# Channel mixing on one core: three of seven block products split once more, three parts per batch by turns, one batch's x in DRAM for a while

## The chip, the cores and the metric

The kernel runs on one core of a Trainium2 chip. The metric is the time of one execution in microseconds on the device. Three runs of the kernel before took 838.82, 838.87 and 838.88 us; the median is 838.87.

## The reference

The input is q, k and v of 4 batches, 8 heads, 768 positions and 64 elements a head, the centroids of 16 clusters per head, and four weights. Attention lets a query see only the keys of its own cluster. Its output, laid out as x of 768 × 512 per batch, goes through a token mixer and a channel mixer:

```python
xt = x.transpose(0, 2, 1)
h = np.maximum(xt @ w_tok1, 0.0) @ w_tok2      # w_tok1 768x256, w_tok2 256x768
u = x + h.transpose(0, 2, 1)
h2 = np.maximum(u @ w_ch1, 0.0) @ w_ch2        # w_ch1 512x1536, w_ch2 1536x512
return (u + h2).astype(np.float32)
```

## The kernel before

The program has three stages, and TensorE (PE) works through all of them.

**Attention** takes 16 steps, one for each pair of heads of a batch. Its code is the same in both kernels.

**Token stage.** It handles two batches at a time (0 and 1, then 2 and 3). `tok1(b, t)` makes the first token product and ScalarE (ACT) writes its relu into `h`. `tok2_chunks` makes the second one as a product of 2 × 2 blocks in Winograd's form: seven block products (p1, p5, c11, u2, c12, c22, c21) in place of eight. The names say which block of the result each completes; blocks A11 to A22 and their sums S1 to S4 are left factors, B11 to B22 and T1 to T4 right ones. Three chains of PSUM banks, X, Z and Y, gather the products, and VectorE (DVE) adds every bank to x after each product. In between, steps of other work are put by hand with `take`: rounding of the last weights (`weight_steps`: load on the SyncE queue SP, two ops on ACT, four on DVE), sums of weights (`left_chunk`), and the turning of u.

**Turning of u.** The channel stage needs u transposed. `u_take(b, i)` copies one of eight pieces of x on ACT into `urows` (L612) and issues a DMA transpose into `ucols` on SP (L614). `u_put(i)` copies the result into `uT` on ACT (L625). `urows` and `ucols` have two buffers each. `u_sums` then makes T1 to T4 of u on DVE.

**Channel stage.** It goes through the batches 0, 1, 2, 3. The 1536 hidden channels are two halves of six chunks of 128 (the rows of blocks of w_ch1), and u is two halves of 384 positions. For each batch there are two parts of three chunks. `ch1_chunk` makes the seven products of a chunk: each is two matmuls of 128 × 128 weights with 384 columns (L741). ACT copies p1, p5 and u2 out of PSUM (L749), DVE adds the later products to the copies (L536), ACT makes the relu, and DVE forms the sums S1 to S4 of the hidden values. `ch2_chunk` makes the second channel product from three chunks of hidden values: seven products of three matmuls with 256 columns each (L792), DVE adding seven times. `chunk` orders the seven products of both functions and leaves the last one, c21, to be made after the first product of the chunk that follows:

```python
        X = ptile("X", n)
        product(X, "A11", "B11", True)
        if late:
            late.pop()()
        done("p1", X)
```

In batch 0 the sums of the weights (`right_weights`, `left_chunk`) are made between the chunks, and `fits` prepares a check of the value range. Every instruction order is the order of the program: nothing is rescheduled. X and Z have three PSUM banks each, Y has two.

A matmul on f32 data appears in the trace as two passes, each with its weight load.

Of the kernel before, what the change touches and what calls it, by code (L numbers as in the profile page):

```python
# [8 lines left out]
F32 = mybir.dt.float32  # L9
# [10 lines left out]
P = 128  # L20
# [16 lines left out]
EX = 9  # L37
SM_SCALE = 0.125
# [10 lines left out]
def kernel(  # L49
# [46 lines left out]
    tokens = fast.enter_context(ExitStack())  # L96
    tokpool = pool("tokpool", 1, tokens)
# [31 lines left out]
    xs = [xpool.tile([P, NJ, DM], F32, name=f"x{b}") for b in range(B)]  # L129
# [401 lines left out]

    def sub(dst, a, b):
        nc.vector.tensor_tensor(out=dst, in0=a, in1=b, op=ALU.subtract)
# [17 lines left out]
    def left_sums(A, part):  # L551
        a = {name: part(x) for name, x in A.items()}
        yield lambda: add(a["S1"], a["A21"], a["A22"])
        yield lambda: sub(a["S2"], a["S1"], a["A11"])
        yield lambda: sub(a["S3"], a["A11"], a["A21"])
        yield lambda: sub(a["S4"], a["A12"], a["S2"])

    def left_chunk(c):
        return left_sums(pools["A"], lambda x: x[:, :, c * P : (c + 1) * P])

    def token_weights():
# [8 lines left out]
        return left_sums(A, lambda x: x)  # L570
# [15 lines left out]
    def right_weights(part):  # L586
# [12 lines left out]
        b = {name: x[:, 3 * part : 3 * part + 3] for name, x in pools["B"].items()}  # L599
# [7 lines left out]
    def u_take(b, i):  # L607
# [3 lines left out]
        rows = pools["u"].tile([P, 2, HJ, P], U16, name="urows", bufs=2)  # L611
        nc.scalar.copy(out=rows, in_=x.rearrange("p j (c w) -> p w j c", w=2))  # L612
        cols = pools["u"].tile([P, 2, HJ, P], U16, name="ucols", bufs=2)
# [13 lines left out]
    def u_steps(b):  # L627

        N = 2 * NF
        for i in range(2):  # L630
            yield lambda i=i: u_take(b, i)
        for i in range(N):
            yield lambda i=i: (u_put(i), i + 2 < N and u_take(b, i + 2))

    def u_sums(half):
        if half == 0:
            uT = pools["uT"]
            uTs = pools["uTs"] = pools["u"].tile([P, 3, NF // 2, HS], F32, name="uTs")
            R = pools["R"] = {
                f"B{i + 1}{j + 1}": uT[:, j, 2 * i : 2 * i + 2] for i in range(2) for j in range(2)  # L640
            }
            R["T1"], R["T2"], R["T4"] = (uTs[:, i] for i in range(3))
            R["T3"] = R["B12"]
            sub(R["T1"], R["B12"], R["B11"])
            sub(R["T2"], R["B22"], R["T1"])
        else:
            R = pools["R"]
            sub(R["T3"], R["B22"], R["B12"])
            sub(R["T4"], R["B21"], R["T2"])

    late, outs = [], []

    def chunk(n, product, done, last):

        X = ptile("X", n)
        product(X, "A11", "B11", True)
        if late:
            late.pop()()
        done("p1", X)
        Z = ptile("Z", n)  # L660
        product(Z, "S1", "T1", True)
        done("p5", Z)
        Y = ptile("Y", n)

        def product_y():
            product(Y, "A12", "B21", True)
            done("c11", Y)

        def product_z():
            product(Z, "S4", "B22", False)  # L670
            done("c12", Z)


        between = [product_y, product_z]
        if not last:
            between.pop(0)()
        product(X, "S2", "T2", False)
        done("u2", X)
        between.pop(0)()
        product(X, "S3", "T3", False)  # L680
        done("c22", X)
        if last:
            between.pop(0)()

        def end():
            product(X, "A22", "T4", False)
            done("c21", X)

        late.append(end)

    def tok2_chunks(b, half):


        A, R = pools["AT"], pools["RT"]
        kinds = {
            "p1": ("X", "A11", "B11", "c11"),
            "p5": ("Z", "S1", "T1", "c22"),
            "c11": ("Y", "A12", "B21", "c11"),
            "u2": ("X", "S2", "T2", "c12"),
            "c12": ("Z", "S4", "B22", "c12"),  # L700
            "c22": ("X", "S3", "T3", "c22"),
            "c21": ("X", "A22", "T4", "c21"),
        }

        def product(name, i):
            tag, a, r, to = kinds[name]
            start = name in ("p1", "p5", "c11")
            if start:
                banks[tag, i] = ptile(tag, DM)
            nc.tensor.matmul(  # L710
                banks[tag, i], lhsT=A[a][:, i], rhs=R[r], start=start, stop=True,
                skip_group_check=not start,
            )
            x = xs[b + int(to[2]) - 1][:, HJ * (int(to[1]) - 1) + i]
            add(x, banks[tag, i], x)

        orders = (
            (("p1", "012"), ("p5", "012"), ("c11", "01"), ("u2", "012"), ("c12", "01")),
            (("c22", "012"), ("c12", "2"), ("c11", "2"), ("c21", "012")),
        )  # L720
        if half == 0:
            pools["banks"] = {}
        banks = pools["banks"]
        for name, chunks in orders[half]:
            for i in chunks:
                product(name, int(i))

    def ch1_chunk(part, i):

        c = 3 * part + i  # L730
        if i == 0:
            pools["h2"] = {
                k: pools["mlp"].tile([P, 3, HS], F32, name="h" + k)
                for k in ("A11", "A12", "A22", "S1", "S2", "S3", "S4")
            }
        A, R, h2 = pools["A"], pools["R"], pools["h2"]
        kept = {}

        def product(psum, a, r, start):
            for k in range(2):  # L740
                nc.tensor.matmul(  # L741
                    psum, lhsT=A[a][:, k, c * P : (c + 1) * P], rhs=R[r][:, k],
# [3 lines left out]
        def done(name, psum):  # L746
            if name in ("p1", "p5", "u2"):
                kept[name] = pools["mlp"].tile([P, HS], F32, name=name, bufs=2)
                nc.scalar.copy(out=kept[name], in_=psum)  # L749
            elif name == "c11":  # L750
                a = h2["A11"][:, i]
                add(a, psum, kept["p1"])
                nc.scalar.activation(out=a, in_=a, func=ACT.Relu)
            elif name == "c12":
                kept["c12"] = pools["mlp"].tile([P, HS], F32, name="c12", bufs=2)
                add(kept["c12"], psum, kept["u2"])
            elif name == "c22":
                a = h2["A22"][:, i]
                add(a, psum, kept["p5"])
                nc.scalar.activation(out=a, in_=a, func=ACT.Relu)  # L760

                nc.vector.scalar_tensor_tensor(
                    out=h2["S3"][:, i], in0=kept["c12"], scalar=0.0, in1=h2["A11"][:, i],
                    op0=ALU.max, op1=ALU.subtract,
                )
                nc.vector.scalar_tensor_tensor(
# [182 lines left out]
    for b in (0, 2):  # L949
# [17 lines left out]
        if b == 2:  # L967
            take(turning, 2)
# [11 lines left out]
        if b == 2:  # L980
            u_sums(0)
# [256 lines left out]
```

## Time and profile before

| | |
|---|---|
| median of three runs | 838.87 us |
| the profiled execution: its time, its span | 838.82 us, 837.0 us |
| busy: PE, weight loads, DVE, ACT | 827.9, 502.6, 518.4, 377.3 us |
| token stage, first `tok1` to last `tok2_chunks` | about 316.6 to 394.7 us |
| channel stage, PE | about 394.7 to 831.3 us |
| matmul pass of 384, 256, 512 columns, mean duration | 487, 379, 593 ns |
| granted TensorE clock | full speed |

The busy times are sums over one execution. A matmul's duration in the trace holds its way through the array as well, so passes overlap; the distance between the starts of two passes says what a pass costs. Lines such as L536 (`add`) and L533 (`sub`) belong to helpers, so the tiles tell which step is meant: `hA`, `hS` are hidden values, `uTs` sums of u, `w1s` and `w2s` sums of w_ch1 and w_ch2, `h1s` sums of the token stage's hidden values.

### The profile page before, as it was taken

How to read it: one execution, taken by the hardware profiler on the slowest of the kernel's cores; microseconds unless marked ns; L12 is line 12 of the kernel's file. 1: busy time of each engine (PE TensorE's matmuls, PEld its weight loads, DVE VectorE, ACT ScalarE, POOL GpSimd, SP SyncE). 2: the span in 40 equal slices, each digit the busy share in tenths (PEclk: the TensorE clock that was granted, in tenths of full speed). 3: DMA queues.
4: the chain of work that ended last, by engine and by line, in shares of the span. 5: the costliest groups of instructions: out<-in, count | busy, mean ns of one | idle time of the engine just before them, and what ended most of it. 6: DMA issues, size and time to landing. Idle time of an engine off the chain costs nothing.

```text
span 837.0 us, 10822 instructions
## 1 busy us (share of the span) xinstructions
PE 827.9 (99%) x4087; PEld 502.6 (60%) x4087; DVE 518.4 (62%) x908; ACT 377.3 (45%) x575; POOL 30.7 (4%) x28
## 2 busy tenths in 40 slices
PE   9999999999999999999999999999999999999997
PEld 4444444444444444444587686785866858768676
DVE  6879898989898878759644735424354234443342
ACT  5678677787877774054201352103612036120210
POOL 1001010101101000000000000000000000000000
PEclk9999999999999999999999999999999999999999
DMA  9886566867676335032000040001410012200001
GB/s 153 147 158 147 117 139 130 165 131 160 145 136 130 83 95 152 18 88 39 0 1 1 19 107 25 1 1 19 95 39 0 1 20 52 80 0 1 1 19 61
DMA packets 183965, 60.21 MB, mean 72 GB/s; under 512 B 172768, under 2 KB 176864, under 8 KB 183904
## 3 DMA queue, kind: packets, MB, share of 16 engines
q1 hardware_dynamic: 182304, 59.04, 33.5%
q8 instruction: 34, 0.56, 0.3%
q10 hardware_dynamic: 1600, 0.39, 0.2%
q14 instruction: 27, 0.22, 0.1%
HBM read 34.64 MB, written 6.29 MB: 49 GB/s over the span
## 4 chain that ended last, share of the span: by engine, by line
PE 93%; DVE 5%; issue 0%; DMA 0%; ACT 0%; SPq 0%; DVEq 0%; ACTq 0%
PE sc L414 17%; PE pX L792 15%; PE pX L741 14%; PE av L439 13%; PE pZ L741 8%; PE pZ L792 7%; PE ph L518 5%; PE pY L792 4%; PE pY L741 4%; PE pX L710 2%; PE small L475 1%; DVE sum L429 1%; PE pZ L710 1%; PE small L299 1%; DVE x L536 1%; PE pY L710 1%
## 5 line engine op out<-in xcount | busy, mean ns | idle before, releaser
L421 ACT ACTIVATE ex<-sc 128x768 f32<-128x768 f32 x192 | 151.0, 812 | 28.5 <-PE sc L414 16.9
L414 PE MATMUL sc<-qkT 64*128 64x384 f32 x768 | 155.0, 482 | 0.0
L429 DVE TENSOR_TENSOR sum<-sum,ex 128x768 f32<-128x768 f32 x128 | 127.8, 999 | 26.9 <-ACT ex L421 14.2
L439 PE MATMUL av<-ex,va 128*64 128x384 f32 x768 | 127.4, 488 | 0.0
L439 PEld LDWEIGHTS av<-ex,va 128*64 128x64 f32 x768 | 53.7, 137 | 71.7 <-issue 67.5
L414 PEld LDWEIGHTS sc<-qkT 64*128 64x128 f32 x768 | 67.9, 187 | 38.4 <-issue 38.3
L749 ACT COPY p<-pX 128x384 f32<-128x384 f32 x24 | 11.4, 475 | 134.9 <-PE pX L741 117.4
L741 PE MATMUL pX<-uT,wc 128*128 128x384 f32 x192 | 67.3, 487 | 0.2 <-DVE x L536 0.2
L414 PE MATMUL sc<-ohT 64*128 64x384 bf16 x384 | 62.7, 323 | 0.1
L536 DVE TENSOR_TENSOR x<-pX,x 128x512 f32<-128x512 f32 (+1 forms) x48 | 25.8, 553 | 44.3 <-PE pX L792 42.8
L741 PEld LDWEIGHTS pX<-uT,wc 128*128 128x128 f32 x192 | 36.3, 190 | 24.7 <-issue 1.0
L446 ACT COPY avrows<-av 128x768 uint16<-128x768 uint16 x32 | 25.5, 797 | 45.0 <-PE av L439 45.0
L536 DVE TENSOR_TENSOR c<-pZ,u 128x384 f32<-128x384 f32 x24 | 13.4, 558 | 47.3 <-PE pZ L741 47.3
L518 PE MATMUL ph<-x,wt 128*128 128x512 f32 x96 | 41.6, 593 | 0.0
L625 ACT COPY uT<-ucols 128x768 uint16<-128x768 uint16 x32 | 33.7, 1053 | 17.6 <-DMA ucols<-urows 17.5
L760 ACT ACTIVATE hA<-hA 128x384 f32<-128x384 f32 x24 | 12.5, 523 | 64.0 <-DVE hA L536 64.0
L414 PEld LDWEIGHTS <-ohT 64*128 64x128 bf16 x384 | 18.7, 94 | 34.3 <-issue 9.4
L741 PE MATMUL pZ<-uTs,w1s 128*128 128x384 f32 x96 | 35.3, 490 | 0.6 <-DVE w1s L536 0.2
L792 PE MATMUL pX<-w2s,hA 128*128 128x256 f32 x144 | 35.0, 379 | 0.0
L792 PE MATMUL pX<-wc,hA 128*128 128x256 f32 x144 | 35.0, 379 | 0.0
L792 PE MATMUL pZ<-w2s,hS 128*128 128x256 f32 x144 | 35.0, 379 | 0.0
L792 PE MATMUL pY<-wc,hA 128*128 128x256 f32 x144 | 35.0, 379 | 0.0
(139 smaller groups left out, 1214.3 us busy)
## 6 DMA issues: line engine op xcount, KB each, us to landing
raw<-in_moe_w_ch_dram SPq DMA_DIRECT2D x24, 512.0 KB, 4.6
va<-in_v_dram SPq DMA_DIRECT2D x16, 384.0 KB, 3.6
out_dram<-x SPq DMA_DIRECT2D x24, 256.0 KB, 2.3
qk<-in_k_dram SPq DMA_DIRECT2D x60, 96.0 KB, 3.8
qk<-in_q_dram SPq DMA_DIRECT2D x60, 96.0 KB, 3.6
raw<-in_moe_w_tok_dram SPq DMA_DIRECT2D x3, 512.0 KB, 4.3
raw<-in_moe_w_tok_dram SPq DMA_DIRECT2D x4, 384.0 KB, 3.9
ucols<-urows SPq DMA_TRANSPOSE x32, 2.8
```

The lines of the kernel that those rows point to most:

```text
L414: nc.tensor.matmul(sc[:, h, 0:HS], lhsT=src[rows, 1, j], rhs=src[rows, 0, js], start=start, stop=not start,)
L421: nc.scalar.activation(out=ex, in_=sc[:, :, 0:HS], func=ACT.Exp, scale=SM_SCALE)
L429: nc.vector.tensor_tensor(out=acc, in0=acc if j > 1 else st["ex", qh, 0], in1=st["ex", qh, j], op=ALU.add)
L439: nc.tensor.matmul(av[h * D : (h + 1) * D], lhsT=st["va"][:, h, j], rhs=ex[:, h], start=(j == 0), stop=(j == NJ - 1),)
L446: nc.scalar.copy(out=st["rows"][:, qh], in_=av.bitcast(U16).rearrange("p (t w) -> p w t", w=2))
L518: nc.tensor.matmul(pf, lhsT=W["tok1"][:, j, t * P : (t + 1) * P], rhs=xs[b][:, j], start=(j == 0), stop=(j == NJ - 1),)
L536: nc.vector.tensor_tensor(out=dst, in0=a, in1=b, op=ALU.add)
L625: nc.scalar.copy(out=out, in_=pools.pop(("ucols", i)).rearrange("p w j t -> p w (j t)"))
L710: nc.tensor.matmul(banks[tag, i], lhsT=A[a][:, i], rhs=R[r], start=start, stop=True, skip_group_check=not start,)
L741: nc.tensor.matmul(psum, lhsT=A[a][:, k, c * P : (c + 1) * P], rhs=R[r][:, k], start=start and k == 0, stop=k == 1, skip_group_check=not s ...
L760: nc.scalar.activation(out=a, in_=a, func=ACT.Relu)
L792: nc.tensor.matmul(psum, lhsT=h2[a][:, k, i * P : (i + 1) * P], rhs=Bw[w][:, 3 * part + k], start=start and k == 0, stop=k == 2, skip_grou ...
```

## The change

**Two levels.** The two chunks c and c + 3 of one half are now handled together (`ch1_pair`, with c = part). For every pair but the first of batch 0, three of the seven products, A12·B21, S4·B22 and A22·T4 (called Y, Z and X), are themselves 2 × 2 block products: the two blocks of channels are the two chunks, the inner blocks are the two 128-row halves, and the 384 positions are two times 192. Each is made of seven products of one matmul with 192 columns. The first-level left and right factors get second-level sums: `set_left_sums` (tile `w1ss`, in batch 0 for each part once) and `set_right_sums` (tile `uTss`, for each batch, eight DVE ops). The results are added on DVE to the hidden values, bank by bank; the other four products remain as they were.

**Three parts.** There are three parts per batch, each of one pair, where there were two of three chunks. The second channel product now has two matmuls for each of its products and is made three times per batch (`ch2_chunks`). `by_turns` takes the three rows of blocks by turns, for the token product and the second channel product alike; DVE adds each bank directly to x after each product, 21 times per part.

**Order of the rest.** Small steps (weight sums, second-level sums) come from the list `others`, one after each product (`between`). u is turned in the order 0, 1, 4, 5, 6, 7, 2, 3 with two `urows` and three `ucols`, three takes ahead. In the third part of a batch the next u is turned: three takes in `ch1_pair`, the rest after the fourth product of `ch2_chunks`; T1 follows after the sixteenth, and T2 to T4 and the second-level sums after the last. In the token stage three takes are issued at once where there were two, and `left_sums(0)` works on two chunks where `left_chunk(0)` had one.

**Memory.** The x of batch 1 lies in memory of the token stage. It is written to DRAM before the last `tok1`, and read back into the memory of batch 0's x after batch 0 is out. The channel stage takes the batches in the order 0, 2, 3, 1. The rows of a batch go out after its third part, for the last batch as each is done.

The core of the diff:

```diff
+UROWS, UCOLS = 2, 3
...
-    xs = [xpool.tile([P, NJ, DM], F32, name=f"x{b}") for b in range(B)]
+    spill = spilled.tile([P, NJ, DM], F32, name="spill")
+    xs = [(x1pool if b == 1 else xpool).tile([P, NJ, DM], F32, name=f"x{b}") for b in range(B)]
...
+    def set_lefts():
...
+        both = W["ch1"].rearrange("p f (i r c) -> p f i r c", i=2, r=2)[:, 2:4]
+        single = A["S4"].rearrange("p f (r c) -> p f r c", r=2)
...
+    def set_right_sums():
+        pools["r2"] = pools["w2sums"].tile([P, 3, 3, HS // 2], F32, name="uTss")
+        for blocks in set_rights():
+            yield from winograd_right(blocks)
...
+    def by_turns(n, product, of, done=None, last=False, after=()):
...
+            order = "p1 0 p1 1 p1 2 p5 0 p5 1 p5 2 c11 0 c11 1 u2 0 u2 1 u2 2 c12 0 c12 1 "
+            order += "c22 0 c22 1 c22 2 c12 2 c11 2 c21 0 c21 1 c21 2"
...
+            product(banks[tag, i], a, r, i, name in FIRST)
+            x = of(to, i)
+            add(x, banks[tag, i], x)
...
+            if m in after:
+                after[m]()
+            between()
...
+    def ch1_pair(part, sets, beside):
...
+        def big(psum, a, r, i, start):
+            product(psum, a, r, i, start)
+            between()
+            if a != "A11" and beside:
+                beside.pop(0)()
+
+        def set_(psum, which, name, start):
+            _, a, r, _ = SEVEN[name]
+            nc.tensor.matmul(
+                psum, lhsT=left[which][a][:, part * P : part * P + P], rhs=right[which][r],
+                start=start, stop=True, skip_group_check=not start,
+            )
...
+        def set_x(which, tag, name, x):
+            if tag:
+                chains[which] = ptile(tag, HS // 2)
+            bank = chains[which]
+            set_(bank, which, name, name == "p1")
+            add(x, both(bank) if len(x.shape) == 3 else bank, x)
...
+        if sets:
+            yc = ptile("X", HS)
+            set_(yc[:, n0], "Y", "c11", True)
+            set_(yc[:, n1], "Y", "c12", True)
+            add(a11[:, 0], yc, a11[:, 0])
+            set_x("Y", "Y", "p1", a11[:, 0, n0])
+        Z[1] = ptile("Z", HS)
+        big(Z[1], "S1", "T1", 1, True)
+        nc.scalar.copy(out=p5[:, 1], in_=Z[1])
+        if sets:
+            set_x("Y", None, "u2", a11[:, 0, n1])
+            set_z("Y", ptile("Y", HS // 2), a11)
...
+        big(X[1], "S3", "T3", 1, False)
+        add(a22[:, 1], X[1], p5[:, 1])
+        relu(a22)
+        if sets:
+            set_x("Z", None, "c22", c12[:, 1].rearrange("p (k t) -> p k t", k=2))
+            set_(X[0][:, n0], "X", "c11", False)
+            set_(X[0][:, n1], "X", "c12", False)
+            nc.scalar.copy(out=a12[:, 0], in_=X[0])
+            set_(X[1][:, n0], "X", "c21", False)
+            nc.scalar.copy(out=a12[:, 1], in_=X[1])
...
+            set_x("X", "Y", "p1", a12[:, 0, n0])
+            sum_1()
+
+            def late_1():
+                set_x("X", None, "u2", a12[:, 0, n1])
+                set_z("X", ptile("Z", HS // 2), a12)
+                sub(h2["S2"], h2["S1"], a11)
...
-            take(turning, 2)
+            take(turning, UCOLS)
             take(weights, 2)
...
-            take(list(left_chunk(0)), 4)
+            take(list(left_sums(0)), 4)
+            nc.sync.dma_start(spill, xs[1])
...
+    batches = (0, 2, 3, 1)
...
+            ch1_pair(part, not first, [turning.pop(0) for _ in turning[:UCOLS]])
...
+            if part == 2 and not last:
+                after[3] = lambda: take(turning, len(turning))
+                after[15] = lambda: next(usums)
+                usums = u_sums()
+            ch2_chunks(b, part, last, after)
+            between(len(others))
...
+            if part == 2 and not last:
+                for _ in range(3):
+                    next(usums)
+                for step in set_right_sums():
+                    step()
+                if n == 0:
+                    xs[1] = xpool.tile([P, NJ, DM], F32, name="x0")
+                    nc.sync.dma_start(xs[1], spill)
```

## The prediction

> **What bounds the kernel now.** I read the page first (shares, slices, chain), then the groups by shape, and then the timeline of each engine around the place where the token stage hands over to the channel stage.
>
> ```profile
> span 837.0 us, 10822 instructions
> ...
> PE 827.9 (99%) x4087; PEld 502.6 (60%) x4087; DVE 518.4 (62%) x908; ACT 377.3 (45%) x575; POOL 30.7 (4%) x28
> ...
> PE   9999999999999999999999999999999999999997
> ...
> PEclk9999999999999999999999999999999999999999
> ...
> PE 93%; DVE 5%; issue 0%; DMA 0%; ACT 0%; SPq 0%; DVEq 0%; ACTq 0%
> ```
>
> PE is busy from start to end at the full clock and is nearly the whole chain. A busy PE is not proof of a full one, so the starts decide:
>
> ```profile
> 396.11 1.45 PE L741 MATMUL pZ<-uTs,w1s 128*128 128x384 f32 x4
> 397.40 1.45 PE L741 MATMUL pY<-uT,wc 128*128 128x384 f32 x4
> ...
> 403.85 1.45 PE L741 MATMUL pX<-uTs,wc 128*128 128x384 f32 x4
> 405.45 1.56 PE L741 MATMUL pZ<-uTs,w1s 128*128 128x384 f32 x4
> 406.84 1.45 PE L741 MATMUL pY<-uT,wc 128*128 128x384 f32 x4
> ...
> 601.05 1.46 PE L792 MATMUL pZ<-wc,hS 128*128 128x256 f32 x6
> 602.34 1.46 PE L792 MATMUL pX<-wc,hS 128*128 128x256 f32 x6
> ```
>
> One f32 matmul of the program shows as two passes. Four passes of 384 columns take 1.29 us from start to start (322.5 ns each), six of 256 columns 1.295 (216 ns): 0.833 ns a column plus 2.5 ns. From batch 1 on no gap breaks this rhythm; in batch 0 four products wait for DVE sums of weights (the one at 405.45 comes 0.31 late, and its first pass takes 0.10 longer). So each nanosecond that PE streams less is won, and each new wait of PE is lost at once.
>
> **What the change takes from PE.** A pair of chunks (c, c+3) took 28 matmuls of 384. In 11 of the 12 pairs the three products A12·B21, S4·B22, A22·T4 (12 matmuls, 24 passes) now become 21 matmuls of 192 columns (42 passes). No row has that width with 128 weight columns; the two rows above give 192 × 0.833 + 2.5 = 162.5 ns. Away go 24 × 322.5 = 7.74 us, in come 42 × 162.5 = 6.83: 0.915 us a pair, **−10.07 us** in all. The listing agrees: 132 matmuls of 384 fewer, 231 of 192 more. The second channel product keeps its 504 matmuls.
>
> Can weights be loaded at that pace? The groups by shape (mean ns of one behind the comma):
>
> ```profile
> L741 PEld LDWEIGHTS pX<-uTs,wc 128*128 128x128 f32 x96 | 18.2, 190 | 11.0
> ...
> L536 DVE TENSOR_TENSOR hA<-pX,p 128x384 f32<-128x384 f32 x24 | 13.4, 558 | 15.9 <-PE pX L741 15.9
> ...
> L773 ACT ACTIVATE hA<-pX 128x384 f32<-128x384 f32 x24 | 11.8, 491 | 30.8 <-PE pX L741 30.8
> ...
> L536 DVE TENSOR_TENSOR x<-pX,p 128x256 f32<-128x256 f32 x24 | 10.2, 425 | 20.9 <-PE pX L792 20.9
> ...
> L533 DVE TENSOR_TENSOR uTs<-uT,uTs 128x768 f32<-128x768 f32 x8 | 7.6, 954 | 0.4
> ```
>
> A load lasts 190 ns, more than 162.5. If that were its occupancy, each of 11 × 42 passes would take 27.5 ns more, +12.7 us. But the late product at 405.45 paid only 0.10 us for an unhidden load before it streamed, so I take the load to occupy about 105 ns and to hide. The Trainium skill (TensorE: Matmul & The Clock Gate, "LDWEIGHTS (loading the stationary operand)") makes a load cost its columns divided by 1.2, an estimate of 107 ns for 128 columns: by the rule nothing is added, by the 190 ns row 12.7 us, and no run here shows which holds at 192 columns.
>
> **DVE and ACT prices.** DVE ops follow each other at 0.337 us (256 elements), 0.475 (384), 0.595 (512), 0.87 (768), by the starts of back-to-back adds; for 192 the same slope gives 0.27, lasting 0.36. One that needs the op before it waits about 0.12 longer. DVE or ACT starts 0.20 us after PE's last pass has streamed (402.56 to 402.76). PE streams 0.16 after what it waited for (0.05 to the weight load, 0.105 for it). In a pair with its second product DVE has some 21 us of work (21 adds of 256, 19 ops of 192 to 768) in 35 us of PE time (8 × 1.29 + 21 × 0.325 + 21 × 0.864): not a bound, but chains through it can be late.
>
> **Token stage, batches 2 and 3.** The timeline of ACT, then that of DVE (start, us, what; in brackets the wait before it):
>
> ```profile
> 361.18 1.55 ACT L612 COPY urows<-x 128x768 uint16<-128x768 uint16 x2
> ...
> 368.84 0.67 ACT L202 ACTIVATE wh<-raw 128x512 f32<-128x512 f32 x1 [2.45 <-DMA raw<-in_moe_w_ch_dram]
> ...
> 374.47 0.59 ACT L522 ACTIVATE h<-ph 128x512 f32<-128x512 f32 x1
> ```
>
> ```profile
> 375.09 0.69 DVE L533 TENSOR_TENSOR h1s<-h,h 128x512 f32<-128x512 f32 x1 [3.11 <-ACT h L522]
> ...
> 381.23 1.88 DVE L536 TENSOR_TENSOR x<-pX,x 128x512 f32<-128x512 f32 x3
> ...
> 395.71 0.94 DVE L533 TENSOR_TENSOR uT<-uT 128x768 f32<-128x768 f32 x1
> ```
>
> Now three take steps stand at 361.18 with two urows buffers, so the third copy waits for the first transpose to land: issued 362.03, 2.8 us, 364.83. Behind it on ACT stand the four weight roundings and the relus of h. On SP the two raw weight loads (364.68) stand behind the third transpose (about 365.7 plus 1.27 us issue): 367.0, +2.35. They landed 4.2 us after issue, so the later roundings and with them the relu at 374.47 and DVE's first token sum come 2.35 later. From 375.09 to 397.5 DVE has no gap of note: it sets the pace there. It also gets left_sums of 512 elements where there were 256: 4 × 0.26 = 1.04. The last token adds, whose banks the first channel products wait for, come **3.4 us** later. Bounds: 0 (ACT's wait absorbed) to 5 (loads slower behind three transposes).
>
> The spill (1.5 MB) stands on SP before the last three transposes. At the 434 GB/s that DMA reached between 367 and 368 us, during a raw load, it takes 3.6 us, at the attention stage's 150 GB/s 10. Those transposes feed T2 of u, which DVE reaches after 14 of 21 token products, some 12 us on; ACT has nothing else to do meanwhile. I take 0; with the cover gone, up to 3. The reload waits on SP for batch 0's six rows; the next transpose on SP is 70 us away: 0. Batch order, the later rows of the first three batches and the last row's way out (one 256 KB row after the last add, 2.3 us, as now) cost nothing, ±0.5.
>
> **First pair of batch 0** (old products). Its two A22·T4 products run between the first products of the second part, and those reuse their banks at once: 0.20 to ACT, 0.49 relu, 0.16 back to PE, 0.85 twice, +1.7. In return the four waits for weight sums go (0.31 to 0.37 plus 0.10 each, −1.7), since those sums are now spread between products. **0**; bounds −1.7 and +1.7.
>
> **Batch boundaries, three.** From the end of PE's last product of a batch DVE does that add (start +0.20, next op +0.53), T2, T3, T4 of u (2.61), eight set sums (4 × 0.475 + 4 × 0.27, two or three dependent waits: 3.2), and only at +6.3 the add of the first set bank; two dependent adds end at +7.29, so u2 of that chain can stream at +7.45. PE meanwhile has four large products and three set matmuls before that u2, 4 × 1.29 + 3 × 0.325 = 6.14 us; then it waits, and all later products wait behind it. Stall 1.31, **+3.9 us**; bounds 0.5 and 2 each. Today's boundary has only T1 to T4 there and no wait.
>
> **Within a pair.** The last chain is tight: after the second S3·T3 product 0.20, add 0.56, relu of 768 0.74, copy 0.49, add 0.36, 0.16 and four hand-overs of 0.03: 2.6. PE has five set matmuls and one second-part product, 5 × 0.325 + 0.864 = 2.49. About 0.08 each, **+0.9 us** over 11 pairs; bounds 0 and 0.4 each. The other chain links have 0.4 us or more of room. **Extra weight sums** in batch 0 (24 small DVE ops behind which bank adds queue): **+0.5**, bounds 0 and 2.
>
> Sum: −10.07 + 3.4 + 0 + 3.9 + 0.9 + 0.5 = −1.4. The profiled execution took 838.82 us (span 837.0 and 1.8 around it), the median of the three runs is 838.87; so 837.4.
>
> **Rivals.** (1) *The waits are mostly hidden*: the late token sums are caught up and the boundary costs 0.5 each: −10.07 + 1 + 1.5 + 0.9 + 0.5 = about −6 at best, −4 in the middle, 834.9. For it: DVE is only 62% busy. Against: both waits stand in one engine's own order. (2) *DVE's chains pace the pairs*, ending slower: every set bank is read by DVE before its next product may add to it. If a link of the last chain is 0.1 us longer and the boundary 0.5, it is 11 × 0.3 + 1.5 more, +3.4, 842. It decides once the links after S3·T3 add up to over 2.8 us. For it: the margin is already gone. (3) *The load of 190 ns binds*: −1.4 + 12.7, 850. Against: the 0.10 us of the late product. (4) *Fewer passes do not appear* (the new products replace others, or DMA for the spill takes PE's time): the listing excludes the first.
>
> **How the numbers follow.** About 0.2% (1.7 us) is what a measurement of this kernel can tell from no change. The sum as worked, 0.62, own range 835.4 to 839.6: the forecast lies just inside no change, so 0.24 of it is faster and 0.36 same, 0.02 slower. Rival 1, 0.18, nearly all faster. Rival 2, 0.14, slower with 0.03 same. Rival 3 and others, 0.06, slower. Together faster 0.42, same 0.39, slower 0.19. The range reaches to rivals 1 and 2 and leaves out rival 3: 833.9 to 841.6.
>
> **What would show it.** Right: 192-column passes 162 to 163 ns apart; PE's last stretch ending near 830; waits of PE near 380 (2 to 3 us, on DVE's x adds), three of 1.3 on hA adds at the batch changes, two of 0.85 on ACT in the first pair. Wrong: passes 190 apart, PE gaps of 0.3 or more in every pair, no wait near 380, or a tail longer than now's 6 us after PE.

## The result, and the profile after

The changed kernel takes 838.86 us (median of six runs, 838.69 to 839.02), the kernel before 838.85 beside it: a ratio of 1.0002, 95% interval 0.9989 to 1.0015. That is no difference that can be measured here. The profiled execution took 838.92 us with a span of 837.0; the forecast of 837.4 was 1.5 us too low.

The page of the kernel after, at the places shown of the kernel before (span; busy times; chain that ended last):

```profile
span 837.0 us, 11463 instructions
...
PE 820.4 (98%) x4285; PEld 526.1 (63%) x4285; DVE 606.3 (72%) x1124; ACT 381.3 (46%) x562; POOL 30.7 (4%) x28
...
PE 86%; DVE 7%; ACT 2%; DMA 2%; issue 1%; SPq 0%; ACTq 0%; DVEq 0%
```

PE is busy 7.5 us less in the same span, and its share of the chain fell from 93% to 86%: DVE, ACT and DMA have taken its place on the path. Where, the waits of PE from 370 us on say (engine, line <- releaser: us in total, times, longest):

```profile
PE pY L801 <- DVE hA L554: 3.3, 3, 1.1
PE pX L762 <- DVE x L554: 2.2, 2, 2.0
PE pX L940 <- ACT hA L925: 1.2, 2, 0.6
PE pX L788 <- DVE x L554: 0.5, 1, 0.5
PE pX L940 <- ACT hA L886: 0.4, 1, 0.4
PE pX L762 <- ACT h L527: 0.2, 1, 0.2
```

In this kernel L801 is a matmul of 192 columns, L788 one of 384, L940 the second channel product, L762 the token product, L554 the bank add, L925 the relu of the old-style pair. This view counts a wait from the modelled end of the pass before it. The distance of the starts gives the whole loss, as in PE's timeline after a change of batch:

```profile
512.22 0.49 PE L801 MATMUL pY<-uT,wc 128*128 128x192 f32 x2
512.54 1.45 PE L788 MATMUL pZ<-uTs,w1s 128*128 128x384 f32 x4
515.10 0.92 PE L801 MATMUL pY<-uTss,w1ss 128*128 128x192 f32 x4 [1.11 <-DVE hA L554]
515.85 1.45 PE L788 MATMUL pX<-uTs,w1s 128*128 128x384 f32 x4
```

Two passes of 192 columns take 0.325 us from start to start (512.22 to 512.54), 162.5 ns each, as forecast. Four passes of 384 take 1.29, so the product at 515.10 was due at 513.83: 1.27 late, and its four passes take 0.75 in place of 0.65. I take the 0.10 for a weight load that nothing hid: the first two loads start there at 515.10 and 515.21, although each row lasts 0.19. By such starts, the sum of the prediction against the trace:

| step | forecast, us | in the trace of after |
|---|---|---|
| stream, 11 pairs | −10.07 | passes 162.5 ns apart in every pair |
| token stage | +3.4 | first channel product at 398.27, before 394.75: +3.5, of which 0.13 come from attention, which ends later |
| first pair | −1.7 + 1.7 | the four waits on weight sums are gone; two waits of 0.74 + 0.10 on ACT |
| three batch changes | +3.9 | 3 × (1.27 + 0.10) = 4.1 |
| last chain of a pair | +0.9 | 10 × 0.06 = 0.6 (the eleventh pair is the row before the last) |
| extra weight sums | +0.5 | 0.31 + 0.10 at 465.03 and 0.06 at 458.89 |
| start of the last second product | – | 0.56 + 0.08, at 811.26 where 810.70 was due |
| tail after PE | 0 ± 0.5 | last DVE add to end of span 5.91, before 5.28: +0.6 |

PE's last pass starts at 830.22, before at 830.92, so 0.7 us were won on PE, and the tail gave 0.6 of them back. The two last rows of the table, 1.3 us that the forecast had at nothing, are the error; the other rows miss by 0.3 or less each, and these misses cancel.

The token stage's two parts stand in DVE's rows, first of the kernel before, then of the one after:

```profile
377.96 0.42 DVE L536 TENSOR_TENSOR w1s<-wc 128x256 f32<-128x256 f32 x1
...
379.42 0.68 DVE L533 TENSOR_TENSOR h1s<-h,h1s 128x512 f32<-128x512 f32 x1
```

```profile
377.55 0.69 DVE L551 TENSOR_TENSOR h1s<-h,h 128x512 f32<-128x512 f32 x1 [3.14 <-ACT h L527]
...
380.41 0.68 DVE L554 TENSOR_TENSOR w1s<-wc 128x512 f32<-128x512 f32 x1
...
382.94 0.68 DVE L551 TENSOR_TENSOR h1s<-h,h1s 128x512 f32<-128x512 f32 x1
...
384.75 1.88 DVE L554 TENSOR_TENSOR x<-pX,x 128x512 f32<-128x512 f32 x3
```

The first token sum starts 2.46 later than before (377.55, 375.09), 2.33 without the 0.13 of attention, where the forecast has 2.35. The sums of w_ch1 take 2.53 in place of 1.46, 1.07 more (forecast 1.04), and the first x add comes 3.52 later (384.75, 381.23).

### The profile page after: what moved, and what is told of

It is laid out like the page before. It is cut to its first block, busy times and chain, and to the rows that moved or that the text cites. A ratio compares the mean times of both kernels' runs of the same rounds, so it can differ in the third digit from the quotient of the medians.

```text
span 837.0 us, 11463 instructions
## 1 busy us (share of the span) xinstructions
PE 820.4 (98%) x4285; PEld 526.1 (63%) x4285; DVE 606.3 (72%) x1124; ACT 381.3 (46%) x562; POOL 30.7 (4%) x28
## 4 chain that ended last, share of the span: by engine, by line
PE 86%; DVE 7%; ACT 2%; DMA 2%; issue 1%; SPq 0%; ACTq 0%; DVEq 0%
PE sc L419 19%; PE av L444 14%; PE pX L940 13%; PE pX L788 11%; PE pZ L940 6%; PE pY L801 4%; PE pY L940 3%; PE ph L523 3%; PE pZ L788 3%; PE pZ L801 3%; DVE x L554 2%; PE pX L801 2%; DMA ucols<-urows 1%; PE small L480 1%; PE pX L762 1%
## 5 line engine op out<-in xcount | busy, mean ns | idle before, releaser
L554 DVE TENSOR_TENSOR x<-pX,x 128x256 f32<-128x256 f32 (+1 forms) x168 | 76.2, 459 | 41.2 <-PE pX L940 39.7
L828 ACT COPY hA<-pX 128x384 f32<-128x384 f32 x24 | 11.5, 479 | 147.8 <-PE pX L788 143.0
L554 DVE TENSOR_TENSOR hA<-pY,hA 128x192 f32<-128x192 f32 (+1 forms) x90 | 36.7, 408 | 54.1 <-PE pY L801 39.6
L810 ACT ACTIVATE hA<-hA 128x768 f32<-128x768 f32 x35 | 29.5, 844 | 87.1 <-DVE hA L554 87.1
L788 PE MATMUL pX<-uT,wc 128*128 128x384 f32 x192 | 68.0, 487 | 0.5 <-DVE x L554 0.5
L788 PEld LDWEIGHTS pX<-uT,wc 128*128 128x128 f32 x192 | 35.7, 190 | 18.3 <-issue 1.3
L554 DVE TENSOR_TENSOR x<-pZ,x 128x256 f32<-128x256 f32 (+1 forms) x84 | 36.4, 456 | 13.0 <-PE pZ L940 12.5
L940 PE MATMUL pX<-wc,hA 128*128 128x256 f32 x144 | 37.2, 381 | 1.6 <-ACT hA L925 1.2
L940 PE MATMUL pY<-wc,hA 128*128 128x256 f32 x144 | 35.1, 379 | 0.0
L940 PE MATMUL pZ<-wc,hS 128*128 128x256 f32 x144 | 35.0, 379 | 0.0
L788 PE MATMUL pX<-uTs,w1s 128*128 128x384 f32 x96 | 34.9, 486 | 0.0
```

Source lines behind the costliest of these rows:

```text
L554: nc.vector.tensor_tensor(out=dst, in0=a, in1=b, op=ALU.add)
L788: nc.tensor.matmul(psum, lhsT=A[a][:, k, c], rhs=R[r][:, k], start=start and k == 0, stop=k == 1, skip_group_check=not start,)
L810: nc.scalar.activation(out=x, in_=x, func=ACT.Relu)
L940: nc.tensor.matmul(psum, lhsT=h2[a][:, k, i * P : (i + 1) * P], rhs=Bw[w][:, part + 3 * k], start=start and k == 0, stop=k == 1, skip_grou ...
```

## The experiments

Each kernel is the changed one with one edit, unless said otherwise; times are medians, ratios are against runs of the kernel before on the same chip, whose medians lay between 838.56 and 838.85.

**Two takes first** (`e1_two_takes`).

```diff
-            take(turning, UCOLS)
+            take(turning, 2)
...
-                take(turning, 4)
+                take(turning, 5)
```

> The changed kernel, but with two take steps of u before the last weight roundings of the token stage, as before the change, and the third one after them. Theory (the gain of the stream is real and named waits give it back): the third urows copy no longer waits 2.14 us on ACT for the first transpose, the two raw weight loads are issued on SP about 2.4 us earlier (364.7 instead of 367.2), DVE's first token sum starts near 375.1 instead of 377.55, PE's wait of 2.17 near 382.9 all but vanishes, and the time falls by 2.2 to 2.5 us, to about 836.5. Rival: something else than this wait makes the token stage late (DVE's own queue, or the spill): the sums start earlier but PE's wait on the x adds stays, and the time falls by at most 1.2, to 837.7 or more. A second rival, that the stage is late because the loads themselves are slower: nothing moves, 838.9.

It took 837.38 us, ratio 0.9983 (0.9974 to 0.9992); the first channel product starts at 397.08, 1.2 earlier. That is the size of the first rival, and the reason is in the timelines of ACT and DVE:

```profile
375.00 0.83 ACT L684 COPY urows<-x 128x768 uint16<-128x768 uint16 x1 [0.28 <-DMA ucols<-urows]
375.74 1.10 ACT L527 ACTIVATE h<-ph 128x512 f32<-128x512 f32 x2
```

```profile
376.36 0.69 DVE L551 TENSOR_TENSOR h1s<-h,h 128x512 f32<-128x512 f32 x1 [4.29 <-ACT h L527]
```

The wait of 2.14 is gone and the roundings run 2.4 earlier (368.92 in place of 371.27), but the edit puts five steps of u between them and the relu, where the kernel before has four: one copy more (375.00), with its own 0.73 and a new wait of 0.28. So only half of the term went. With four steps there (the second line of the edit left out, in the kernel with all edits below) the sum starts at 375.20, 2.35 before the 377.55 of the changed kernel, which is the forecast's term.

**Sums of w_ch1 into DVE's gap** (`e2_left_sums_early`).

```diff
         tok1(b + 1, 0)
+        if b == 2:
+            left_weights()
+            take(list(left_sums(0)), 4)
         token_sums(b, 0)
...
-            left_weights()
-            take(list(left_sums(0)), 4)
             nc.sync.dma_start(spill, xs[1])
```

> The changed kernel, but the four sums of w_ch1 for the first part are issued on DVE just before the first token sum of batches 2 and 3 instead of behind it; DVE idles 3.14 us there. Theory: the four sums of 512 elements take 4 x 0.6 = 2.4 us out of the queue between the token sums and the x adds, PE's waits near 382.9 to 397.2 (together 3.9 us with their load shares) shrink, and the first channel product starts up to 2.4 us earlier: time about 836.5. Rival: ACT's relu of the hidden values is what is late and PE would wait for that in place of DVE: the channel stage starts at most 0.5 earlier, 838.4 to 838.9.

836.03 us, ratio 0.9968 (0.9956 to 0.9980). PE's wait of 2.17 (ahead of the pass at 385.49 in the changed kernel) is gone; one of 0.53 + 0.10 on ACT's relu, ahead of the pass at 377.90, and the small ones at the end of the stage (0.66 at most) stay. The theory holds: what stood in DVE's queue between the token sums and the x adds was on the path, all 2.4 us of it.

**The batch change** (`e3_boundary`). DVE's timeline there, in the changed kernel:

```profile
507.90 0.42 DVE L554 TENSOR_TENSOR x<-pX,x 128x256 f32<-128x256 f32 x1 [0.44 <-PE pX L940]
508.24 0.95 DVE L551 TENSOR_TENSOR uTs<-uT,uTs 128x768 f32<-128x768 f32 x1
...
513.77 0.35 DVE L551 TENSOR_TENSOR uTss<-uTs,uTss 128x192 f32<-128x192 f32 x1
514.03 0.55 DVE L554 TENSOR_TENSOR hA<-pX,hA 128x384 f32<-128x384 f32 x1
514.69 0.36 DVE L554 TENSOR_TENSOR hA<-pY,hA 128x192 f32<-128x192 f32 x1
```

From the last add of the batch (507.90) to the first add of a set bank (514.03) DVE works without a gap for 6.1 us, with the hand-over of 0.20 ahead of it the forecast's 6.3. The bank that waits there was complete at 512.22, and PE waits for the add at 514.69.

```diff
-                for _ in range(3):
-                    next(usums)
-                for step in set_right_sums():
-                    step()
+                next(usums)
+                sets = list(set_right_sums())
+                for step in sets[:4]:
+                    step()
+                next(usums)
+                pools["rest"] = [lambda u=usums, s=sets[4]: (next(u), s())] + sets[5:]
...
+        others.extend(pools.pop("rest", []))
         big(X[0], "S2", "T2", 0, False)
```

> The changed kernel, but at the three batch changes DVE makes T2, the four second-level sums that need no T, and T3 only; T4 and the four sums made of it follow one by one after the products of the next batch's first pair. Theory: about 2.3 us of DVE work leave the queue ahead of the first set-bank add, so the three waits of 1.27 + 0.10 us on that chain (513.5, 620.9, 728.3) vanish: 3 x 1.37 = 4.1 us, time about 834.8. Rival (DVE's chains pace the pairs): the work put off lands between the set-bank adds, and PE waits there instead: at most 1.5 us of the 4.1 are won, 837.4 or more, with new waits of 0.3 to 1 us on hA or c adds in these pairs.

In this order T3 and T4 read blocks of u that the second-level sums have already replaced, so the values differ from the reference's; the instructions and their sizes do not. 834.44 us, ratio 0.9949 (0.9936 to 0.9963), 4.1 us below the kernel before. The three waits are gone and no other has come. DVE's total work is the same as before the edit: it was its place that cost. (The kernel with all edits has an order that keeps the values: T2, T3, T4, two of the sums, the other six later.)

**The old-style pair** (`e4_first_pair`).

```diff
-            late.extend([lambda: late_(0), lambda: late_(1)])
+            late_(0)
+            late_(1)
```

> The changed kernel, but in the one pair that is made the old way the two products A22 x T4 are made at the end of the pair instead of between the first products of the second channel product. Theory: the two bank waits on ACT's relu (0.74 + 0.10 us each at 415.65 and 418.65) vanish since other products lie between the reading of a bank and its next use: 1.7 us, time about 837.2. Rival: the moved products wait for DVE's reading of the banks they add to, or the second channel product then waits for the hidden sums: the waits move and less than 0.6 is won, 838.3 or more.

836.97 us, ratio 0.9979 (0.9970 to 0.9988). Both waits are gone and none replaces them, so the two bank waits were worth the 1.7 us.

**The register loads** (`e6_check_load`). The wait before the last second product is put down to ACT's copy by the profile. The source view of line 988, where each engine loads the outcome of the range check into registers, and PE's timeline show what else stands there:

```profile
L988 PEldq TENSOR_LOAD <-count x3: 305/306/496, 809.9 to 810.9; - x3
```

```profile
810.37 0.49 PE L801 MATMUL pY<-uTs,wc 128*128 128x192 f32 x2
811.26 1.10 PE L940 MATMUL pX<-wc,hA 128*128 128x256 f32 x4 [0.40 <-ACT hA L886]
```

```diff
             nc.scalar.copy(out=a11[:, i], in_=X[i])
+        if load:
+            pools["both"] = fits_load()
...
-            if last:
-                both = fits_load()
```

> The changed kernel, but the three register loads by which each engine reads the result of the range check are issued in the last pair after its second product instead of after the pair. Theory: the wait of PE before the last second channel product (0.56 + 0.08 us at 810.5) is the three loads in PE's own queue (0.50, 0.31 and 0.31 us with 0.1 between, 1.33 together), which stood behind an instruction held by a semaphore until about 809.8 and had only about 0.8 us of issued work ahead of them; between two large products of 1.29 us they hide, the wait falls to the 0.06 of every other pair or to nothing, and the time falls by 0.5, to 838.4. Rival: the profile's releaser, ACT's copy of hA behind the long relu, is the cause: the wait stays, 838.9, or the loads hold PE at the new place for up to 0.6.

838.19 us, ratio 0.9994 (0.9985 to 1.0003). The interval alone doesn't tell it from no change; the trace does (L942 is the second channel product here):

```profile
810.52 0.49 PE L801 MATMUL pY<-uTs,wc 128*128 128x192 f32 x2
810.84 1.03 PE L942 MATMUL pX<-wc,hA 128*128 128x256 f32 x4
811.70 0.55 PE L801 MATMUL pY<-uTss,w1ss 128*128 128x192 f32 x2
```

At that place the passes now follow each other without a gap, the pair's usual 0.06 is back (0.55 in place of 0.49), and no wait appears at the new place. In the kernel before the same loads ran from 818.88 to 820.20 and cost nothing: PE had issued work until 820.78, and the product behind them started then, on time. The diff doesn't change the loads, it moves them, from ahead of the last third of the second channel product to ahead of the whole of it (not among the lines shown above), and the forecast gave the move no price: they had lost their cover.

**The tail** (`e5_last_order`, `e10_last_order_2`, `e11_one_dma`). The last output row's DMA takes 1.10 us to issue on SP after the change; before, the longest of these was 0.57 and the last 0.33.

```diff
 # first other order
-p1 0 p1 1 p1 2 p5 0 p5 1 p5 2 c11 0 c11 1 u2 0 u2 1 u2 2 c12 0 c12 1 c11 2 c12 2 c22 0 c22 1 c21 0 c22 2 c21 1 c21 2
+p1 0 p1 1 p5 0 p5 1 u2 0 u2 1 c11 0 c11 1 c12 0 c12 1 c22 0 c22 1 p1 2 c21 0 c21 1 p5 2 u2 2 c11 2 c22 2 c12 2 c21 2
 # second other order: the end
+... c22 0 c22 1 p1 2 c21 0 u2 2 p5 2 c22 2 c21 1 c21 2 c11 2 c12 2
```

> The changed kernel, but the last second channel product of the program is made in another order: two rows of blocks of each half first, the third ones last, so that the output rows are ready after products 9, 10, 14, 15, 20 and 21 of 21 instead of 12, 13, 15, 18, 20 and 21. Theory: the last row's DMA took 1.10 us to issue on SP where all others took 0.33, since too many rows were on their way; with earlier rows it takes 0.33 again, the tail after PE's end goes from 6.6 back to about 5.9 us and the time falls by 0.7 to 0.8, to 838.1. Rival: the long issue belongs to the last two rows, which are still 0.86 us apart: nothing moves, 838.9; or the other order brings a wait of PE of up to 0.8 us, 838.9 to 839.7.

838.59 us, ratio 0.9999 (0.9990 to 1.0008): nothing moved, the last issue takes 0.92, as the first rival said.

> The changed kernel, but the last second channel product ends with the products c21 1, c21 2, c11 2, c12 2, so that rows are ready after products 9, 10, 14, 18, 19 and 21 of 21 and the last row comes 1.73 us after the one before it. If the long last issue on SP (1.10 us, 0.92 with the first other order, 0.33 in the kernel before, where the last two rows are 1.29 apart) comes from a row still on its way 0.86 us before, it is 0.33 here and the tail after PE's end falls by 0.6 to 0.8 (time 838.1). If it comes from the place in the queue (the 265th DMA), it stays at 0.7 to 1.1 us and the time stays at 838.9.

838.60 us, ratio 0.9999 (0.9990 to 1.0009). The last issue is short again (0.33), the one before it, 0.86 us after its predecessor, takes 0.83; but the time doesn't fall. SP's waits say where it went, first in the changed kernel, then here (L1359 is the closing branch):

```profile
SPq L1359 <- SPq L1359: 2.7, 1, 2.7
```

```profile
SPq L1359 <- SPq L1359: 3.5, 1, 3.5
```

```diff
-            for j in range(NJ):
-                out_row(j)
+            nc.sync.dma_start(out[b].rearrange("(p j) m -> p j m", p=P), xs[b])
```

> The changed kernel, but the six output rows of each batch except the last go out as one DMA of 1.5 MB instead of six of 256 KB; the last batch's rows stay as they are. The last row's DMA is then the 250th on SP's queue instead of the 265th, with the same bytes ahead of it. If the number of DMAs on the queue makes its issue long, it takes 0.33 us here and the time falls by 0.6 to 0.8, to 838.1; if the distance of 0.86 us to the row before it or the bytes passed do, it stays at 0.7 to 1.1 us and the time at 838.9.

838.87 us, ratio 1.0001 (0.9992 to 1.0011), last issue 1.10: the number of DMAs ahead of it isn't it. (The count of 265 has four that ACT issues; on SP alone the last row is the 261st, here the 246th.) Issue and closing wait together are 3.8 us after the change (1.10 + 2.7), 4.0 and 3.8 with the other orders (0.92 + 3.1, 0.33 + 3.5), 3.1 in the kernel before (0.33 + 2.8). Between the kernel before and the one after, the issue is what grew, by 0.77, while the wait is 0.15 shorter. Nine traces have the changed kernel's order of the last rows. In them the wait is 2.6 to 2.9 us whatever the issue takes, and the tail goes with the issue: from the last add to the end of the span 5.5 to 5.8 us with issues of 0.71 to 0.76, 5.9 to 6.2 with 1.00 to 1.13, against 5.28 in the one trace of the kernel before. But a short last issue alone wins nothing: with the second other order the last row lands 4.0 us after its issue starts, 2.6 to 3.1 in all other traces, and the closing wait ends 0.02 us after that landing.

What makes the issue long no run tests. The distance of 0.86 us is not enough, since an earlier row 0.86 us after another takes 0.33 (824.18 in the changed kernel). The traces show a candidate: on the DMA queue that the profile lists as `q8 instruction`, a transfer of 16 KB runs across the long issue in all 13 traces that have one, and the issue ends 0.35 to 0.40 us after it. In the kernel before that transfer ends at 831.65, just ahead of the last row's issue at 831.79; with the second other order it falls on the row before the last. Why the last row lands so late there stays open.

**Spill twice** (`e9_spill_twice`).

```diff
             nc.sync.dma_start(spill, xs[1])
+            nc.sync.dma_start(spill, xs[1])
```

> The changed kernel, but the x of batch 1 is written to DRAM twice, one write after the other, ahead of the last three transposes on SP. Theory: the spill costs nothing because T2 of u, which needs the last transpose, is reached by DVE at 394.17, 3.5 us after the last copy into uT ended (390.7). A second write takes 3.6 to 5.9 us (at 434 GB/s, or the 5.9 us that the first took), so T2 comes 0.1 to 2.4 late and DVE holds up the x adds behind it: the time rises by 0 to 2.4, most likely about 1, 839.9. Rival 1: the spill is on the path already: the time rises by the whole 3.6 to 5.9, 842.5 to 844.8. Rival 2: the writes and the transposes go side by side: nothing moves, 838.9. On the side: the last row's DMA, 265th on the SP queue in all kernels with a long last issue (0.73 to 1.10 us), is the 266th here; if its place in the queue makes it long, another one is long.

838.64 us, ratio 0.9997 (0.9988 to 1.0007): nothing moved, at the lower end of the theory. But the second rival's reason is false too, since the transposes did wait (ACT, then DVE):

```profile
392.10 0.83 ACT L684 COPY urows<-x 128x768 uint16<-128x768 uint16 x1 [9.73 <-DMA ucols<-urows]
392.84 1.96 ACT L697 COPY uT<-ucols 128x768 uint16<-128x768 uint16 x2
```

```profile
394.42 0.96 DVE L551 TENSOR_TENSOR uTs<-uT,uTs 128x768 f32<-128x768 f32 x1
```

ACT's idle time grew from 2.94 to 9.73 and the copies into uT came 7 us later, yet T2 starts at 394.42 (394.17 in the changed kernel). I had the cover wrong: T2 needs only the first of the last three transposed pieces, whose copy now ends at about 393.9; the other two feed T4, which comes at 400. The cover was some 7 us, not 3.5, and the doubled spill used nearly all of it. The last row's issue is long here too (0.74), with one DMA more ahead of it.

**A sum at the wrong place** (`e12_sum_first`).

```diff
+            sum_1()
             set_x("X", "Y", "p1", a12[:, 0, n0])
-            sum_1()
```

> The changed kernel, but in every pair DVE makes the hidden sum S1 (0.95 us, 768 elements) just before the first bank add of the last set chain instead of just behind it. DVE's load stays the same. Theory (the chain after the second S3 x T3 product has no room, however idle DVE is on average): the sum can start when ACT's relu ends, 0.4 us before that add starts now, and keeps DVE for 0.87, so the add comes about 0.5 us later and PE's wait of 0.06 in each pair becomes about 0.55: 10 or 11 x 0.5, the time rises by 4.5 to 5.5 us to about 843.8. Rival (such links have cover; DVE is 73% busy and idles 0.8 us just there): the idle time takes it, below 840.

843.24 us, ratio 1.0054 (1.0037 to 1.0071), 4.4 above the changed kernel. The same view of PE's waits:

```profile
PE pY L801 <- DVE hA L554: 6.3, 13, 1.1
```

Thirteen waits where there were three: ten pairs now wait 0.46 + 0.10 each in place of 0.06, 10 × 0.5 = 5.0, less 0.4 that a later wait in batch 0 got shorter. So this chain is as tight as the forecast's 2.6 against 2.49 us said, and rival 2 was a matter of tenths.

**All edits together, with and without the second level** (`e7_all_fixed`, `e8_all_fixed_one_level`).

```diff
-            take(turning, UCOLS)
+            take(turning, 2)
...
-                for step in set_right_sums():
-                    step()
+                sets = list(set_right_sums())
+                for step in sets[:2]:
+                    step()
+                pools["rest"] = sets[2:4] + [lambda i=i, s=sets: (s[i](), s[i + 1]()) for i in (4, 6)]
...
+        others.extend(pools.pop("rest", []))
         Z[1] = ptile("Z", HS)
```

The other four edits are those of the runs above: the sums of w_ch1, the old-style pair, the first other order of the last rows, the register loads.

> The changed kernel with six edits together: two takes first and the third only behind the relu of the hidden values (the first experiment had left it ahead of that relu), the sums of w_ch1 before the first token sum, a shorter batch change (T2 to T4, then only the first two second-level sums; the other six follow after the next products), the old-style pair's last products at its end, the other order of the last rows, and the register loads in the last pair. Theory: the named waits of PE go. Token stage 3.5 of its 4.3 us of waits, batch changes 4.1, first pair 1.7, last pair 0.5, tail 0.7: 10.5 us, time about 828.3, so that the whole 10 us by which the stream was shortened show against the kernel before. Rival (the pairs are paced by DVE or by weight loads, or the waits cover one another): waits of the next rank appear and half or less is won, 833 to 836.

828.18 us, ratio 0.9873 (0.9858 to 0.9888), where 828.3 was expected: 10.6 us below the kernel before, and so below the changed kernel, which takes the same time. Its page:

```profile
span 826.5 us, 11464 instructions
...
PE 818.2 (99%) x4285; PEld 526.6 (64%) x4285; DVE 606.1 (73%) x1124; ACT 381.1 (46%) x562; POOL 30.6 (4%) x28
...
PE 96%; DVE 2%; DMA 0%; ACT 0%; issue 0%; SPq 0%; DVEq 0%; ACTq 0%
```

DVE has as much work as before the edits. PE's last pass starts 10.44 us earlier than in the changed kernel: 4.2 of it in the token stage, 3.9 at the batch changes (one still waits 0.08 + 0.10), 1.7 in the first pair, 0.6 in the last. That the total hits the expectation to 0.1 is partly luck: the tail gave nothing of its 0.7 (5.87 us after the last add), and the token stage 0.7 more than its 3.5.

The other kernel of this pair of runs:

```diff
-            ch1_pair(part, not first, [turning.pop(0) for _ in turning[:UCOLS]], last)
+            ch1_pair(part, False, [turning.pop(0) for _ in turning[:UCOLS]], last)
```

> As the kernel with all six edits, but every pair is made the old way, with 12 matmuls of 384 columns in place of 21 of 192; the second-level sums are still made on DVE but nothing reads them. Theory: 11 pairs x (24 x 322.5 - 42 x 162.5 ns) = 10.07 us longer, less 11 x 0.06 of waits that only the second level has: 9.4 us above the kernel with all six edits, about 837.7. Rival (narrow passes do not pay, or DVE's and ACT's extra work around them costs what they save): within 3 us of the kernel with all six edits.

Here the unused second-level sums replace blocks of u and of w_ch1 that the old products read, so its values are not the reference's. 836.97 us, 8.8 above its partner, where 9.4 was expected:

```profile
span 834.8 us, 10885 instructions
...
PE 825.9 (99%) x4087; PEld 502.4 (60%) x4087; DVE 561.3 (67%) x992; ACT 372.2 (45%) x551; POOL 30.7 (4%) x28
```

In the channel stage PE waits nowhere in this kernel but at the end of the range check, which its partner has too; the partner's other waits there sum to 1.35, where the expectation had counted 0.66. From the first to the last pass of that stage the partner takes 8.71 us less (425.70 for 434.40). So the stream itself is 8.71 + 1.35 = 10.06 us shorter with the second level, the 10.07 of the forecast.

## Why the prediction was right, and where not

**The result.** That the change is worth next to nothing was right, and so was the reason: a gain of 10 us on PE, given back by waits that the new order brings. But the 837.4 was 1.4 below the kernel before, and faster had a little more of the chance (0.42) than no change (0.39): that the time did not move at all comes from the 1.3 us that the sum had at nothing. The runs that took the waits away one by one won 1.2, 2.5, 4.1 and 1.6 us against the kernel before, and all of them together 10.6.

**The stream.** Passes of 192 columns follow each other at 162.5 ns, interpolated from 384 and 256 columns, although the load rows still last 190 ns. Rival 3 is refuted, and the late product's 0.10 was the right row to go by. The Trainium skill (TensorE: Matmul & The Clock Gate, "LDWEIGHTS (loading the stationary operand)"), by which 128 columns make an estimate of 107 ns, agrees with this: the late first pass after each batch change loses 0.10.

**Token stage, batch changes, first pair.** The sizes were 3.4 for 3.4, 3.9 for 4.1 and 0 for 0, the last one made of two terms of 1.7 that were both found. The split of the token stage needed two runs, as my first edit undid only half of its term. For the kernel it had one more lesson: the place for the weight sums was a gap of DVE, 3.14 us after the change, that stood with 3.11 us in the rows of before.

**The last chain.** 0.06 for 0.08 a pair, ten times. The 0.08 doesn't follow from its own links, though: as written they add up to 2.63, which against 2.49 would make 0.14 a pair. The trace has 2.55.

**Spill.** The 0 was right and its reason half wrong: I let T2 wait for all the late transposes, while it needs only the first of them. The error was on the safe side.

**Where it failed.** The step "the last row's way out costs nothing, ±0.5" was too small by 0.1 at its end: the tail cost 0.6, and one of the named signs of being wrong, a tail longer than now's, is there. My price, one row of 2.3 us after the last add as now (the median of all rows; the last one took 2.8 before and 3.0 after), looked at the data and not at SP's own issue and closing wait, 3.1 us before and 3.8 after. And the wait ahead of the last second channel product (811.26) was no step at all. Three loads of 0.5, 0.3 and 0.3 us stood in PE's queue in the kernel before as well; I listed what the diff adds to each queue, but not what it moves there to a place with less work in front.

**The rivals.** Rival 1 (waits mostly hidden) is refuted: the waits showed at their full price. Rival 2 (DVE's chains pace the pairs) didn't happen at 0.06, but the misplaced sum shows that it begins at once. The first half of rival 4 is excluded by PE's count of passes, 4285 for 4087: 2 × (231 − 132) = 198 more; the second, that DMA for the spill takes PE's time, by the doubled spill, with which nothing moved.

## What to carry to other kernels

Where one engine is full, a change that shortens its stream has to be priced together with every queue that feeds it: here 10 us were won and 10 were lost, most of them to the order of a few instructions on DVE and ACT, and came back when these were moved, small sums into a gap that the trace already showed. An engine's share of busy time says nothing on this: DVE is 72% busy in the changed kernel and 73% in the one with all edits. What counts is what stands in its queue between the producer and the one add that the full engine waits for. List also the instructions that a change only moves, if less work stands in front of them at the new place.

## What was unexpected of the hardware

- Three register loads from memory hold PE's own queue for 1.3 us (0.50, 0.31 and 0.31 with 0.1 between) and cost 0.56 where about 0.8 us of issued matmuls lay ahead of them; the profile's releaser for that wait was ACT, as such loads are not counted as busy.
- The issue of a 256 KB row of the last batch takes SP 0.33 us, but 0.71 to 1.13 where a 16 KB transfer of the queue `q8 instruction` runs across it (13 traces; that the transfer is the cause is not shown). With the second other order the last issue was short, but its row landed only 4.0 us after that issue started, and the time stayed.
- A weight load of 128 columns still lasts 190 ns by its rows while passes are 162.5 ns apart. After a wait the second load starts 0.11 us after the first, and the first pass loses 0.10.
